# Block-masked attention with a mixture of experts: the scores of twelve attention units as three products of parts on 64 rows of the array per head

## Chip, cores and metric

The kernel runs on one core of one Trainium2 chip. The metric is the device time of one execution in microseconds (us), given as the median of several runs.

## What is computed

Block-masked attention over q, k and v of shape (4, 8, 576, 64): four batches, eight heads, 576 positions, 64 elements per head. The result, 2304 tokens of 512 features, goes through four experts that all work on every token, each with its own weight in the sum.

```python
scores = q @ k.T / sqrt(64)              # per batch and head, 576 x 576
mask = (pos_i // 64) >= (pos_j // 64)    # a query sees the keys of its own and earlier 64-blocks
attn = softmax(where(mask, scores, -1e9))
x = (attn @ v), heads side by side       # 2304 x 512
p = domain_probs / (sum(domain_probs) + 1e-9)
out = sum over e of p[:, e] * (relu(x @ w1[e]) @ w2[e])   # w1 512 x 1024, w2 1024 x 512
```

Everything is float32 outside. Inside, most products run on values that are split into two parts: a copy rounded to the type fp32r, the high part, and what the subtraction leaves, the low part. A product is then the sum of high by high, high by low and low by high.

## The kernel before, in words

**Order of the work.** Nothing is scheduled by hand. Each piece of work is a Python generator that asks for buffers and yields operations with a cost, an engine (or a choice of ACT and DVE) and a priority; `Flow.run` (line 212) takes the operation that can start first by these estimated times and appends it to its engine's program. So the order on each engine is fixed when the program is built, and at run time an engine waits in line for whatever its next instruction needs. An operation marked `late(..., by)` (line 382) is put later by a lag: `LAG_FIRST` 800 ns or `LAG` 3000 ns, so that TensorE doesn't reach it before its operands are there. The PE takes matmuls of the experts (`mm1` at line 1196, L1210; `mm2` at line 1238, L1261) between the operations of attention.

**Attention units.** After a first block of 64 queries per batch (`first_block`) there are 16 units (`unit`, line 455): four per batch, each with two heads, 512 queries (64 to 575) and 576 keys. The first four, those of batch 0, are "plain": their scores are float32 products with each head on 64 rows of the array, head 0 in partitions 0 to 63, head 1 in 64 to 127 (line 587). A float32 product leaves two passes in the trace. The twelve later units, "split", are what the change is about. Scores are made transposed, keys on the partitions and queries along the free axis, in pieces of 128 keys, each for the queries that see them: 512, 448, 320 and 192 queries wide, and 64 for the last 64 keys.

**Scores of a split unit before.** The k of both heads is turned by DVE into kT, head 0 in the upper half of the partitions and head 1 in the lower (L482). `k_thread` writes from it the tile KK: for each head, 128 rows of which 64 hold the high part of k and 64 the low part (lines 490 to 498). q is loaded twice, so that both halves of the partitions hold the same head, turned (L516) and split into HH (high) and LL (low), 1024 columns for two heads (lines 524 and 525). A piece is then two products on all 128 rows: KK by HH and KK by LL (lines 599 and 600), which add up high and low of k by high and low of q. The last 64 keys of both heads are one further product of 128 columns (lines 648 and 649). Each goes to one of two PSUM banks named att; the masked corners are overwritten with a large negative number (ACT L546 or DVE L548), then ACT or DVE copies the bank to the tile S (L703, L409), DVE takes the maximum into cm (L416), and the bank is free.

**After the scores.** GpSimd reduces cm over the partitions (L771), DVE subtracts, ACT takes the exponential (L727), DVE adds up the pieces, GpSimd sums over the partitions (L750). The products with v of two units run together (L825), in column halves of the array, into both att banks. The result is scaled, split and written to the experts' input x, or for the last two batches kept raw in the tiles xr, from which `prepare` (line 1315) makes the operands (A22, S3, S2, S1, S4) of the last two blocks. These two blocks are done in one go with a seven-product scheme (L1650, L1535).

Of the kernel before, what the change touches and what calls it, by code (L numbers as in the profile page):

```python
# [8 lines left out]
F32 = mybir.dt.float32  # L9
# [253 lines left out]
def kernel(  # L263
# [78 lines left out]
    for tag, n, shape, dt in (  # L342
        ("kr", 2, [P, S], F32),
        ("qr", 1, [P, 2 * MAXW], F32),
        ("kT", 1, [P, S], F32),
        ("qT", 1, [P, 2 * MAXW], F32),
        ("KK", 2, [P, 2 * S], F32R),
        ("HH", 1, [P, 2 * MAXW], F32R),
        ("LL", 1, [P, 2 * MAXW], F32R),
        ("VN", 2, [P, (MASK_BLOCK + MAXW) // P + 1, 3, D], F32),  # L350
        ("tr", 1, [P, MAXW], F32),
        ("tc", 1, [P, MAXW // 8], F32),
        ("S", 2, [P, 2 * MAXC], F32),
        ("cm", 1, [P, 2 * MAXW], F32),
        ("mx", 1, [P, 2 * MAXW], F32),
        ("sa", 1, [P, 2 * MAXW], F32),
        ("sb", 1, [P, 2 * MAXW], F32),
        ("xs", 2, [P, MAXW], F32),
        ("rc", 1, [P, MAXW], F32),
    ):  # L360
        bufs(tag, n, shape, dt, attn)
        counts[tag] = n
# [92 lines left out]
    def unit(u, ua, us, ju, pu, ph, job, dst, c):  # L455
        b, q0, q1 = job
        W = q1 - q0
        nt, odd = q1 // P, (q1 // MASK_BLOCK) % 2
# [9 lines left out]
        def k_thread():  # L468
# [16 lines left out]
            if plain:  # L485
                st["k"] = (kT, [t], [t])
                return
            KK = yield fl.take("KK", us)
            kt, kk = kT.tile, KK.tile
            a1 = yield a_copy(kk[0:64, :q1], kt[0:64, :q1], q1, [t], [kT, KK], pr)  # L490
            l1 = yield tt(BOTH, kk[64:128, :q1], kt[0:64, :q1], kk[0:64, :q1], SUB, q1, [a1], [kT, KK], pr)
            rot = MASK_BLOCK * odd
            second = []
            for to, of, n in ((q1 + rot, 0, q1 - rot), (q1, q1 - rot, rot)):
                if n:
                    second.append((yield a_copy(kk[64:128, to:to + n], kt[64:128, of:of + n], n, [t], [kT, KK], pr)))
                    second.append((yield tt(BOTH, kk[0:64, to:to + n], kt[64:128, of:of + n], kk[64:128, to:to + n],
                                            SUB, n, second[-1:], [kT, KK], pr)))
            fl.give(kT)
            st["k"] = (KK, [a1, l1], second)  # L500

        def q_thread():
# [4 lines left out]
            for h, j in ((h, j) for h in range(2) for j in range(2 if plain else 4)):  # L507
                p0, c0 = (64 * h + 32 * j, 0) if plain else (32 * j, h * W)
                vals.append((yield dma(
                    qr.tile[p0:p0 + 32, c0:c0 + W].rearrange("c (i r) -> c i r", r=32),  # L510
                    q[b, h0 + h, q0:q1, 32 * (j % 2):32 * (j % 2) + 32].rearrange("(i c) r -> c i r", c=32),
                    W * 128, u=[qr], prio=pr, packet=128)))
            yield ("until", lambda: left_first[0] == 0 and past["w"] > 2)
            qT = yield fl.take("qT", ua)
            n = W if plain else 2 * W
            t = yield op("dve", 1.04 * n + 70, lambda _: nc.vector.transpose(out=qT.tile[:, :n], in_=qr.tile[:, :n]),  # L516
                         vals, [qr, qT], pr)
            fl.give(qr)
            if plain:
                st["q"] = (qT, t)  # L520
                return
            HH = yield fl.take("HH", us)
            LL = yield fl.take("LL", us)
# [3 lines left out]
            st["q"] = (HH, LL, a, l)  # L527

        def v_thread():
# [11 lines left out]

        def mask(r, o, m, pb):

            def fn(e):
                if e == "act":
                    nc.scalar.activation(o, ident[r:r + 64, :64], AF.Copy, bias=neg, scale=0.0)  # L546
                else:
                    nc.vector.memset(o, neg)  # L548

            return op([("act", 193.0), ("dve", 120.0)], 0, fn, [m], [pb], pr - 1.0)  # L550

        banks = []
        for h in range(2):
            cur, used = [], 0
            for pc in pcs:
                if pc[0] is None and not plain:
                    continue
# [7 lines left out]
        if plain:  # L565
            banks.sort(key=lambda x: (x[1][0][0], x[0]))
        elif odd:
            banks.append((None, [pcs[-1]]))

        def s_thread():  # L570
# [6 lines left out]
            KK, ka, kb = st["k"]  # L577
            lag = LAG_FIRST if plain else LAG
            if plain:
                qT, qv = st["q"]  # L580
                Q = [qT]
                need = lambda h: ka + [qv]
                cost = lambda w: 2 * max(107.0, 2 * w / 2.4 + 2.5)

                def product(o, h, k0, n, lo):
                    hp = slice(64 * h, 64 * h + 64)
                    nc.tensor.matmul(out=o, lhsT=KK.tile[hp, k0:k0 + n], rhs=qT.tile[hp, lo:W], start=True, stop=True)  # L587
            else:
                HH, LL, qa, ql = st["q"]
                Q = [HH, LL]  # L590
                Hv = HH.tile[:, :2 * W].rearrange("p (h w) -> p h w", h=2)
                Lv = LL.tile[:, :2 * W].rearrange("p (h w) -> p h w", h=2)
                need = lambda h: (ka + kb if h is None else kb if h else ka) + [qa, ql]
                cost = lambda w: 2 * max(85.0, w / 2.4 + PEO)

                def product(o, h, k0, n, lo):
                    at = k0 + (q1 + MASK_BLOCK * odd) * h
                    hs = h
                    nc.tensor.matmul(out=o, lhsT=KK.tile[:, at:at + n], rhs=Hv[:, hs, lo:W], start=True, stop=False)  # L599
                    nc.tensor.matmul(out=o, lhsT=KK.tile[:, at:at + n], rhs=Lv[:, hs, lo:W], start=False, stop=True)  # L600

            for h, ps_list in banks:
                if plain:

                    if h:
                        continue
                    two = []
                    for _ in range(2):
                        two.append((yield fl.take("att", None, bank_tag)))

                    def fn(_, two=two, ps_list=ps_list):
                        at = 0
                        for j, a, w, _ in ps_list:
                            for g in range(2):
                                product(two[g].tile[:, at:at + w], g, q1 - P if j is None else P * j, P, a - q0)
                            at += w

                    ws = [x[2] for x in ps_list]
                    m = yield late(op("pe", 300.0 + (2 * sum(ws) + ws[0] - sum(abs(x - y) for x, y in zip(ws, ws[1:]))) / 1.2,
                                 fn, need(0), [*two, KK] + Q, pr), lag)  # L620
                    for g in range(2):
                        done, at, spots = [m], 0, {}
                        for j, a, w, _ in ps_list:
                            r = 64 if j is None else 128 if a == P * j else None
                            if r:
                                spots.setdefault(r, []).append(at)
                            at += w
                        for r, x in spots.items():
                            o = two[g].tile[r - 64:r, x[0]:x[0] + 64]
                            if len(x) == 2:  # L630
                                o = two[g].tile[r - 64:r, x[0]:2 * x[1] - x[0]].rearrange("p (n w) -> p n w", n=2)[:, :, :64]
                            i = ident[r - 64:r, :64 * len(x)]
                            i = i.rearrange("p (n w) -> p n w", n=2) if len(x) == 2 else i
                            done.append((yield op("act", 0.833 * 64 * len(x) + 140, lambda _, o=o, i=i: nc.scalar.activation(
                                o, i, AF.Copy, bias=neg, scale=0.0), [m], [two[g]], pr)))
                        st["banks"].append((g, ps_list, two[g], done))
                    continue
                pb = yield fl.take("att", None, bank_tag)
                ps = pb.tile
                use = [pb, KK] + Q  # L640
                done = []
                if h is None:
                    lo = W - MASK_BLOCK
                    n = 2 * MASK_BLOCK

                    def fn(_, ps=ps, n=n, lo=lo):
# [1124 lines left out]
```

## Time and profile before

| | |
|---|---|
| median of 3 runs | 880.06 us (879.18 to 880.15) |
| the profiled execution | 879.1 us, of it 877.3 us from its first to its last instruction |
| TensorE busy | 868.6 us of 877.3 |
| VectorE, ScalarE, GpSimd busy | 804.7, 551.0, 224.8 us |
| granted TensorE clock | 1.0 throughout |

Engines are PE (TensorE's matmuls), PEld (its weight loads), DVE (VectorE), ACT (ScalarE), POOL (GpSimd) and SP. A matmul's start is recorded, its end is modelled, so that successive matmuls overlap in the trace: the time that one costs is the step from its start to the start of the next, not its duration. In a form such as `64*128 64x512 f32` the first pair is the rows and columns of the array in use, the second the partitions and columns of the moving operand. fp32r is shown as f32 on PE.

### The profile page before, as it was taken

To read this page: it belongs to the slowest core of one execution; us is meant where nothing else is said; L and a number is where in the kernel's file an instruction comes from. 1 tells how busy PE (TensorE), PEld (TensorE's weight loads), DVE (VectorE), ACT (ScalarE), POOL (GpSimd) and SP (SyncE) were. 2 spreads that over 40 slices of the span, in tenths; PEclk is the share of its full clock that TensorE was granted. 3 is DMA by queue.
4 is the path that set the end of the run, shared out by engine and by line. 5 is a ranking of instruction groups with operands and counts; after the bars stand their busy time and mean duration, and the time that the engine had idled before them with its cause. 6 is when DMAs were issued, how large, how long until landed. Compare 5 with 4: busy or idle time off the path is not lost.

```text
span 877.3 us, 14545 instructions
## 1 busy us (share of the span) xinstructions
PE 868.6 (99%) x4965; PEld 729.1 (83%) x4967; DVE 804.7 (92%) x1489; ACT 551.0 (63%) x1183; POOL 224.8 (26%) x149
## 2 busy tenths in 40 slices
PE   8999999999999999999999999999999999999998
PEld 6777788878877887887887887889999999999998
DVE  6999999898898988988998789999999999999988
ACT  6696767765655564765764652585857677584852
POOL 1141100412412322232232322000061514334150
PEclk9999999999999999999999999999999999999999
DMA  7877457635455356356525223223383947575485
GB/s 172 220 183 213 133 129 194 167 125 122 97 125 140 81 132 147 110 135 149 111 66 152 65 89 91 85 82 112 96 127 69 142 79 125 94 137 72 74 125 165
DMA packets 231179, 108.10 MB, mean 123 GB/s; under 512 B 128448, under 2 KB 212416, under 8 KB 231104
## 3 DMA queue, kind: packets, MB, share of 16 engines
q1 hardware_dynamic: 215264, 93.13, 40.0%
q0 software_dynamic: 13824, 12.59, 12.0%
q10 hardware_dynamic: 2016, 1.44, 0.5%
q8 instruction: 39, 0.64, 0.3%
q14 instruction: 36, 0.29, 0.1%
HBM read 87.72 MB, written 19.40 MB: 122 GB/s over the span
## 4 chain that ended last, share of the span: by engine, by line
PE 95%; SPq 1%; ACT 1%; DMA 1%; issue 0%; DVE 0%; DVEq 0%; ACTq 0%
PE acc L1261 25%; PE h L1210 25%; PE acc L1535 18%; PE h L1650 10%; PE att L1650 8%; PE att L825 5%; PE att L600 2%; PE att L599 2%; SPq L394 1%; PE acc L587 1%; DMA qr<-in_q_dram 0%; PE att L587 0%; PE acc L825 0%; DMA w2r<-in_moe_w_dram 0%; DMA S<-in_k_dram 0%
## 5 line engine op out<-in xcount | busy, mean ns | idle before, releaser
L1210 PE MATMUL h<-xh,w1h 128*128 128x512 f32 (+1 forms) x384 | 137.2, 357 | 0.0
L1210 PE MATMUL h<-xh,w1l 128*128 128x512 f32 (+1 forms) x384 | 136.2, 355 | 0.0
L1210 PE MATMUL h<-xl,w1h 128*128 128x512 f32 (+1 forms) x384 | 136.0, 354 | 0.0
L750 POOL PARTITION_ALL_REDUCE sb<-sa x26 | 84.0, 3278 | 171.0 <-DVE tr L865 99.8
L1261 PE MATMUL acc<-w2h,hh 128*128 128x512 f32 x312 | 124.2, 398 | 0.0
L1261 PE MATMUL acc<-w2h,hl 128*128 128x512 f32 x312 | 122.0, 391 | 0.7 <-DVE hl L1230 0.7
L1261 PE MATMUL acc<-w2l,hh 128*128 128x512 f32 x312 | 122.0, 391 | 0.0
L409 ACT CAST w2h<-w2r 128x512 fp32r<-128x512 f32 (+1 forms) x114 | 70.0, 614 | 66.0 <-PE acc L1261 51.9
L771 POOL PARTITION_ALL_REDUCE mx<-cm x16 | 52.8, 3297 | 222.0 <-DVE cm L416 174.9
L1228 ACT ACTIVATE hh<-h 128x512 fp32r<-128x512 f32 (+1 forms) x94 | 49.2, 523 | 66.1 <-PE h L1210 65.8
L416 DVE TENSOR_TENSOR w1l<-w1r,w1h 128x512 fp32r<-128x512 f32 (+1 forms) x128 | 88.7, 695 | 1.9 <-ACT w1h L409 1.1
L403 POOL DMA_DIRECT2D out_dram<-ohp x48 | 42.6, 1393 | 161.2 <-DVE ohp L1571 161.2
L409 ACT CAST w1h<-w1r 128x512 fp32r<-128x512 f32 (+1 forms) x111 | 67.7, 611 | 23.9 <-DMA w1r<-in_moe_w_dram 15.0
L416 DVE TENSOR_TENSOR w2l<-w2r,w2h 128x512 fp32r<-128x512 f32 (+1 forms) x116 | 80.0, 691 | 2.7 <-ACT w2h L409 2.6
L1210 PEld LDWEIGHTS h<-xh,w1h 128*128 128x128 f32 x384 | 72.6, 189 | 11.3 <-issue 0.9
L1210 PEld LDWEIGHTS h<-xl,w1h 128*128 128x128 f32 x384 | 72.6, 189 | 10.2
L1210 PEld LDWEIGHTS h<-xh,w1l 128*128 128x128 f32 x384 | 72.5, 189 | 10.2
L1261 PEld LDWEIGHTS acc<-w2h,hl 128*128 128x128 f32 x312 | 58.6, 188 | 13.9 <-DVE hl L1230 1.2
L1261 PEld LDWEIGHTS acc<-w2h,hh 128*128 128x128 f32 x312 | 58.8, 188 | 13.4 <-issue 1.2
L1230 DVE SCALAR_TENSOR_TENSOR hl<-h,hh 128x512 fp32r<-128x512 f32 (+1 forms) x94 | 55.7, 593 | 13.7 <-ACT hh L1228 13.2
L1261 PEld LDWEIGHTS acc<-w2l,hh 128*128 128x128 f32 x312 | 58.9, 189 | 9.8
L403 POOL DMA_DIRECT2D out_dram<-o x48 | 42.5, 1382 | 76.7 <-DVE o L1571 63.4
(365 smaller groups left out, 2371.6 us busy)
## 6 DMA issues: line engine op xcount, KB each, us to landing
w1r<-in_moe_w_dram SPq DMA_DIRECT2D x120, 256.0 KB, 3.1
w2r<-in_moe_w_dram SPq DMA_DIRECT2D x116, 256.0 KB, 3.0
qr<-in_q_dram SPq DMA_DIRECT2D x112, 64.0 KB, 2.3
out_dram<-ohp POOLq DMA_DIRECT2D x48, 128.0 KB, 4.1
out_dram<-o POOLq DMA_DIRECT2D x48, 128.0 KB, 4.3
kr<-in_k_dram SPq DMA_DIRECT2D x64, 72.0 KB, 2.9
VN<-in_v_dram SPq DMA_DIRECT2D x32, 128.0 KB, 2.7
w2rp<-in_moe_w_dram SPq DMA_DIRECT2D x12, 256.0 KB, 3.4
```

What stands on the lines that cost most here:

```text
L403: o = op("pool", 1400.0, lambda _: nc.gpsimd.dma_start(out=dst, in_=src, accum_op=ALU.add), r, u, prio)
L409: o = op(engs, 0, lambda e: nc.scalar.copy(dst, src) if e == "act" else nc.vector.tensor_copy(dst, src), r, u, prio)
L416: o = op(engs, 0, lambda e: ENG[e].tensor_tensor(out=dst, in0=a, in1=b, op=alu), r, u, prio)
L750: sums.append((yield held(2300.0, op("pool", 150 + 6.3 * W, lambda _, h=h: nc.gpsimd.partition_all_reduce(sb.tile[:, h * W:h * W + W], sa. ...
L771: lambda _: nc.gpsimd.partition_all_reduce(mx.tile[:, :2 * W], src, P, RED.max),
L825: nc.tensor.matmul(out=x.tile[64 * g:64 * g + 64, W - w:W], lhsT=lhsT, rhs=rhs, start=(i == 0), stop=(i == len(todo) - 1))
L1210: nc.tensor.matmul(out=ps[:, :n], lhsT=s.tile[:, ks], rhs=x.tile[:, kc, :n], start=(kc == 0 and m == 0), stop=(kc == KC - 1 and m == 2),)
L1228: a = yield op("act", 0.833 * n + 55, lambda _: nc.scalar.activation(hh.tile[:, :n], ps[:, :n], AF.Relu), [mm], [pb, hh], 0.0)
L1230: l = yield op("dve", 1.04 * n + 70, lambda _: nc.vector.scalar_tensor_tensor(out=hl.tile[:, :n], in0=ps[:, :n], scalar=0.0, in1=hh.tile[: ...
L1261: nc.tensor.matmul(out=acc, lhsT=s.tile[:, ts], rhs=w.tile, start=(f == 0 and m == 0), stop=(f == FC - 1 and m == 2))
L1535: nc.tensor.matmul(out=acc[:, to], lhsT=s.tile[:, ts], rhs=v.tile[:, of], start=(start and first and m == 0 and k % 2 == 0), stop=(what != ...
L1650: nc.tensor.matmul(out=ps[:, :n], lhsT=w.tile[:, ks], rhs=x[:, kc, :n], start=(start and kc == 0 and m == 0), stop=(i in (2, 3, 4) and kc ...
```

## The change

Split units now make their scores the way plain ones do, but with parts. kT is split whole into KH and KL (128 partitions, one head in each half); q is loaded once per head, turned and split into QH and QL, 512 columns instead of 1024. Each piece is three products per head, KH by QH, KL by QH and KH by QL, on the 64 rows of the head; the two heads' products are issued alternately, into two att banks, which are both taken before the first product. The pieces come in the plain order, in three banks per head: 512; 192 and 320; 448 and 64. The last 64 keys become a full piece of 128 keys whose upper half is masked, so the last piece of v is loaded with 128 rows per head. Corners are masked by ACT alone, two in one instruction where a bank has two corners at the same partitions. The joint bank for the last 64 keys is gone.

```diff
 for tag, n, shape, dt in (
-    ("qr", 1, [P, 2 * MAXW], F32), ("qT", 1, [P, 2 * MAXW], F32),
-    ("KK", 2, [P, 2 * S], F32R), ("HH", 1, [P, 2 * MAXW], F32R), ("LL", 1, [P, 2 * MAXW], F32R),
+    ("qr", 1, [P, MAXW], F32), ("qT", 1, [P, MAXW], F32),
+    ("KH", 2, [P, S], F32R), ("KL", 2, [P, S], F32R),
+    ("QH", 2, [P, MAXW], F32R), ("QL", 2, [P, MAXW], F32R),
...
-        pcs, C = pieces_beside(q0, q1) if plain else pieces_of(q0, q1)
+        pcs, C = pieces_beside(q0, q1)
...
-            a1 = yield a_copy(kk[0:64, :q1], kt[0:64, :q1], q1, [t], [kT, KK], pr)
-            l1 = yield tt(BOTH, kk[64:128, :q1], kt[0:64, :q1], kk[0:64, :q1], SUB, q1, [a1], [kT, KK], pr)
...
+            a = yield a_copy(KH.tile[:, :q1], kT.tile[:, :q1], q1, [t], [kT, KH], pr)
+            l = yield tt(BOTH, KL.tile[:, :q1], kT.tile[:, :q1], KH.tile[:, :q1], SUB, q1, [a], [kT, KH, KL], pr)
...
-            for h, j in ((h, j) for h in range(2) for j in range(2 if plain else 4)):
+            for h, j in ((h, j) for h in range(2) for j in range(2)):
...
-            a = yield a_copy(HH.tile[:, :2 * W], qT.tile[:, :2 * W], 2 * W, [t], [qT, HH], pr)
-            l = yield tt(BOTH, LL.tile[:, :2 * W], qT.tile[:, :2 * W], HH.tile[:, :2 * W], SUB, 2 * W, [a], [qT, HH, LL], pr)
+            a = yield a_copy(QH.tile[:, :W], qT.tile[:, :W], W, [t], [qT, QH], pr)
+            l = yield tt(BOTH, QL.tile[:, :W], qT.tile[:, :W], QH.tile[:, :W], SUB, W, [a], [qT, QH, QL], pr)
...
-                r, o, n = (slice(0, P), 2 * h, P) if plain else (slice(64 * h, 64 * h + 64), 1, MASK_BLOCK)
-                jv.append((yield dma(VJ.tile[r, at, o, :], v[b, h0 + h, q1 - n:q1], n * 256, u=[VJ], prio=pr + 0.005, packet=256)))
+                jv.append((yield dma(VJ.tile[:, at, 2 * h, :], v[b, h0 + h, q1 - P:q1], P * 256, u=[VJ], prio=pr + 0.005, packet=256)))
...
+            turns = ((0, 0),) if plain else ((0, 0), (1, 0), (0, 1))
+            def product(two, at, k0, w, lo):
+                for i, (x, y) in enumerate(turns):
+                    for g in range(2):
+                        hp = slice(64 * g, 64 * g + 64)
+                        nc.tensor.matmul(out=two[g].tile[:, at:at + w], lhsT=K[x].tile[hp, k0:k0 + P], rhs=Q[y].tile[hp, lo:W],
+                                         start=(i == 0), stop=(i == len(turns) - 1))
...
-                        m = yield late(op("pe", cost(w), fn, need(h), use, pr), lag)
+                cost = 300.0 + (...) / 1.2 if plain else sum(3 * (x / 2.4 + PEO) for x in ws)
+                m = yield late(op("pe", cost, fn, ka + qv, [*two, *K, *Q], pr), lag)
```

## Rows read from the trace of the kernel before

**Rows 1.** The page: its head and the engines' busy time.

```profile
span 877.3 us, 14545 instructions
PE 868.6 (99%) x4965; PEld 729.1 (83%) x4967; DVE 804.7 (92%) x1489; ACT 551.0 (63%) x1183; POOL 224.8 (26%) x149
```

**Rows 2.** The chain that ended last, share of the span by engine.

```profile
PE 95%; SPq 1%; ACT 1%; DMA 1%; issue 0%; DVE 0%; DVEq 0%; ACTq 0%
```

**Rows 3.** The stretch 130 to 570 us: busy time and count of each engine, clock.

```profile
130.00:570.00 440.00, 440.00 (x2100) 355.23 (x2099) 395.85 (x652) 258.73 (x544) 117.32 (x36) 1.00 0.46 119
```

**Rows 4.** Waits of the weight loads, 130 to 570 us: total us, times, longest.

```profile
PEld acc L1261 <- ACT KK L409: 0.8, 1, 0.8
```

**Rows 5.** The products of all score pieces, by line: count, duration ns, first and last start.

```profile
L599 PE MATMUL att<-HH,KK x96: 251/334/393, 140.1 to 505.3; 128*128 128x512 f32 x24, 128*128 128x448 f32 x24, 128*128 128x320 f32 x24, 128*128 128x192 f32 x24
L649 PE MATMUL att<-LL,KK x12: 275/276/277, 154.5 to 508.3; 128*128 128x128 f32 x12
```

**Rows 6.** The chain in order of time: start us, us, twelve expert products in a row.

```profile
137.50 2.72 PE h L1210 x12
```

**Rows 7.** PE in order of time, first split unit: start us, us, what.

```profile
140.06 0.39 PE L599 MATMUL att<-HH,KK 128*128 128x512 f32 x1
...
141.15 0.40 PE L1261 MATMUL acc<-w2l,hh 128*128 128x512 f32 x1
...
143.65 0.30 PE L599 MATMUL att<-HH,KK 128*128 128x320 f32 x1
...
144.39 0.39 PE L1210 MATMUL h<-xl,w1h 128*128 128x512 f32 x1
...
154.44 0.22 PE L648 MATMUL att<-HH,KK 128*128 128x128 f32 x1
...
154.90 0.39 PE L1261 MATMUL acc<-w2l,hh 128*128 128x512 f32 x1
```

**Rows 8.** PE in order of time around two score groups of plain units.

```profile
61.14 0.39 PE L1261 MATMUL acc<-w2h,hl 128*128 128x512 f32 x1
61.46 1.13 PE L587 MATMUL acc<-qT,kT 64*128 64x192 f32 x8
...
62.86 0.40 PE L1261 MATMUL acc<-w2l,hh 128*128 128x512 f32 x1
...
83.12 0.40 PE L1261 MATMUL acc<-w2h,hl 128*128 128x512 f32 x1
83.44 1.13 PE L587 MATMUL acc<-qT,kT 64*128 64x512 f32 x4
...
85.76 0.39 PE L1261 MATMUL acc<-w2l,hh 128*128 128x512 f32 x1
```

**Rows 9.** Weight loads in order of time, in such a group and around L649.

```profile
83.44 0.30 PEld L587 LDWEIGHTS acc<-qT,kT 64*128 64x128 f32 x4 [0.36 <-ACT rc L844]
83.98 0.19 PEld L587 LDWEIGHTS att<-qT,kT 64*128 64x128 f32 x2 [0.23 <-ACT xs L409]
84.41 0.20 PEld L587 LDWEIGHTS att<-qT,kT 64*128 64x128 f32 x2 [0.23 <-issue]
...
154.55 0.19 PEld L1261 LDWEIGHTS acc<-w2h,hh 128*128 128x128 f32 x1
154.66 0.19 PEld L1261 LDWEIGHTS acc<-w2l,hh 128*128 128x128 f32 x1
```

**Rows 10.** Groups of DVE, 130 to 570 us: count, busy us, mean ns.

```profile
L416 DVE TENSOR_TENSOR LL<-qT,HH 128x1024 fp32r<-128x1024 f32 x12 | 19.0, 1581 | 0.2
...
L416 DVE TENSOR_TENSOR KK<-kT,KK 64x576 fp32r<-64x576 f32 x11 | 10.0, 910 | 0.3
```

**Rows 11.** DMA issues of q: count, KB each, us to landing.

```profile
qr<-in_q_dram SPq DMA_DIRECT2D x112, 64.0 KB, 2.3
```

**Rows 12.** In order of time: when S3l is made on DVE and first read on PE.

```profile
546.76 1.22 DVE L416 TENSOR_TENSOR S3l<-xr,S3h 128x1024 fp32r<-128x1024 f32 x1
...
555.08 0.39 PE L1650 MATMUL h<-S3l,w1hp 128*128 128x512 f32 x1
```

More of the change, by code (lines that the diff above doesn't have):

```diff
@@ L485, in k_thread @@
             if plain:
-                st["k"] = (kT, [t], [t])
+                st["k"] = ((kT,), [t])
                 return
-            KK = yield fl.take("KK", us)
-            kt, kk = kT.tile, KK.tile
-            a1 = yield a_copy(kk[0:64, :q1], kt[0:64, :q1], q1, [t], [kT, KK], pr)
-            l1 = yield tt(BOTH, kk[64:128, :q1], kt[0:64, :q1], kk[0:64, :q1], SUB, q1, [a1], [kT, KK], pr)
[L492 to L498, printed above, removed]
+            KH = yield fl.take("KH", us)
+            KL = yield fl.take("KL", us)
+            a = yield a_copy(KH.tile[:, :q1], kT.tile[:, :q1], q1, [t], [kT, KH], pr)
+            l = yield tt(BOTH, KL.tile[:, :q1], kT.tile[:, :q1], KH.tile[:, :q1], SUB, q1, [a], [kT, KH, KL], pr)
             fl.give(kT)
-            st["k"] = (KK, [a1, l1], second)
+            st["k"] = ((KH, KL), [a, l])
         def q_thread():
@@ L514, in q_thread @@
             qT = yield fl.take("qT", ua)
-            n = W if plain else 2 * W
-            t = yield op("dve", 1.04 * n + 70, lambda _: nc.vector.transpose(out=qT.tile[:, :n], in_=qr.tile[:, :n]),
+            t = yield op("dve", 1.04 * W + 70, lambda _: nc.vector.transpose(out=qT.tile[:, :W], in_=qr.tile[:, :W]),
                          vals, [qr, qT], pr)
@@ L555, in unit @@
             for pc in pcs:
-                if pc[0] is None and not plain:
-                    continue
                 if used + pc[2] > 512:
@@ L564, in unit @@
                 banks.append((h, cur))
[L565 to L568, printed above, removed]
+        banks.sort(key=lambda x: (x[1][0][0], x[0]))
         def s_thread():
@@ L576, in s_thread @@
             st["banks"] = []
-            KK, ka, kb = st["k"]
             lag = LAG_FIRST if plain else LAG
[L579 to L600, printed above, removed]
@@ L602, in s_thread @@
-            for h, ps_list in banks:
[L603 to L636, printed above, removed]
-                    continue
[L638 to L646, printed above, removed]
-                        lhsT = KK.tile[:, q1 - MASK_BLOCK:q1 + MASK_BLOCK]
-                        nc.tensor.matmul(out=ps[:, :n], lhsT=lhsT, rhs=Hv[:, :, lo:W], start=True, stop=False)
-                        nc.tensor.matmul(out=ps[:, :n], lhsT=lhsT, rhs=Lv[:, :, lo:W], start=False, stop=True)
-                    m = yield late(op("pe", 220.0, fn, need(None), use, pr), lag)
-                    m1 = yield mask(64, ps[64:128, 0:64], m, pb)
-                    m2 = yield mask(0, ps[0:64, 64:128], m, pb)
-                    done = [m, m1, m2]
-                else:
@@ new lines, in s_thread @@
+            K, ka = st["k"]
+            Q, qv = st["q"]
+            turns = ((0, 0),) if plain else ((0, 0), (1, 0), (0, 1))
[5 more added lines that the diff above has]
+                                         start=(i == 0), stop=(i == len(turns) - 1))
@@ L656, in s_thread, with fn @@
+            for h, ps_list in banks:
+                if h:
+                    continue
+                two = []
+                for _ in range(2):
+                    two.append((yield fl.take("att", None, bank_tag)))
+                def fn(_, two=two, ps_list=ps_list):
                     at = 0
-                    corners = []
                     for j, a, w, _ in ps_list:
-                        def fn(_, o=ps[:, at:at + w], j=j, h=h, a=a):
-                            product(o, h, P * j, P, a - q0)
-                        m = yield late(op("pe", cost(w), fn, need(h), use, pr), lag)
-                        done = [m]
-                        if a == P * j:
-                            corners.append(at)
-                        at += w
@@ L668, in s_thread @@
-                    for x in corners:
-                        done.append((yield mask(64, ps[64:128, x:x + 64], done[0], pb)))
-                st["banks"].append((h, ps_list, pb, done))
-            fl.give(KK, *Q)
+                        product(two, at, q1 - P if j is None else P * j, w, a - q0)
+                        at += w
+                ws = [x[2] for x in ps_list]
+                cost = 300.0 + (2 * sum(ws) + ws[0] - sum(abs(x - y) for x, y in zip(ws, ws[1:]))) / 1.2 if plain else sum(3 * (x / 2.4 + PEO) for x in ws)
@@ new lines, in s_thread @@
+                m = yield late(op("pe", cost, fn, ka + qv, [*two, *K, *Q], pr), lag)
+                for g in range(2):
+                    done, at, spots = [m], 0, {}
+                    for j, a, w, _ in ps_list:
+                        r = 64 if j is None else 128 if a == P * j else None
+                        if r:
+                            spots.setdefault(r, []).append(at)
+                        at += w
+                    for r, x in spots.items():
+                        o = two[g].tile[r - 64:r, x[0]:x[0] + 64]
+                        if len(x) == 2:
+                            o = two[g].tile[r - 64:r, x[0]:2 * x[1] - x[0]].rearrange("p (n w) -> p n w", n=2)[:, :, :64]
+                        i = ident[r - 64:r, :64 * len(x)]
+                        i = i.rearrange("p (n w) -> p n w", n=2) if len(x) == 2 else i
+                        done.append((yield op("act", 0.833 * 64 * len(x) + 140, lambda _, o=o, i=i: nc.scalar.activation(
+                            o, i, AF.Copy, bias=neg, scale=0.0), [m], [two[g]], pr - (0.0 if plain else 1.0))))
+                    st["banks"].append((g, ps_list, two[g], done))
@@ L673, in e_thread @@
+            fl.give(*K, *Q)
         def e_thread():
@@ L682, in e_thread @@
                 cu = [] if alone else [cm]
-                if h is None:
-                    _, a, w, c0 = ps_list[0]
-                    pv = ps[:, :2 * w].rearrange("p (h w) -> p h w", h=2)
-                    e = yield a_copy(Sv[:, :, c0:c0 + w], pv, 2 * w, done, [pb, Sb], pr, True)
-                    st["evac"].append(e)
-                    if not alone:
-                        base = Sv[:, :, a - q0:W] if len(pcs) == 2 else cv[:, :, a - q0:W]
-                        st["evac"].append((yield tt("dve", cv[:, :, a - q0:W], pv, base, MAX, 2 * w, done + st["evac"],
-                                                    [pb, Sb] + cu, pr)))
-                else:
-                    tot = sum(x[2] for x in ps_list)
-                    c0 = ps_list[0][3]
-                    moves = [(Sv[:, h, c0:c0 + tot], ps[:, :tot])]
-                    r1 = min([x[1] for x in pcs[1:]], default=q0) - q0
-                    if r1 and ps_list[0][0] == 0:
-                        moves.append((cv[:, h, :r1], ps[:, :r1]))
-                    n = tot + r1 * (len(moves) - 1)
-                    def fn(e, moves=moves):
-                        for d_, s_ in moves:
-                            (nc.scalar.copy if e == "act" else nc.vector.tensor_copy)(d_, s_)
-                    e = yield op([("act", 0.833 * n + 60 * len(moves)), ("dve", 1.04 * n + 70 * len(moves))], 0, fn, done,
-                                 [pb, Sb] + cu, pr - (0.0 if plain else 1.0))
-                    st["evac"].append(e)
-                    at = 0
-                    for j, a, w, _ in ps_list:
-                        r = a - q0
-                        if j == 0:
-                            pass
-                        else:
-                            base = Sv[:, h, r:W] if j == 1 else cv[:, h, r:W]
-                            st["evac"].append((yield tt("dve", cv[:, h, r:W], ps[:, at:at + w], base, MAX, w,
-                                                        done + st["evac"], [pb, Sb] + cu, pr)))
-                        at += w
@@ new lines, in e_thread, with fn @@
+                tot = sum(x[2] for x in ps_list)
+                c0 = ps_list[0][3]
+                moves = [(Sv[:, h, c0:c0 + tot], ps[:, :tot])]
+                r1 = min([x[1] for x in pcs[1:]], default=q0) - q0
+                if r1 and ps_list[0][0] == 0:
+                    moves.append((cv[:, h, :r1], ps[:, :r1]))
+                n = tot + r1 * (len(moves) - 1)
+                def fn(e, moves=moves):
+                    for d_, s_ in moves:
+                        (nc.scalar.copy if e == "act" else nc.vector.tensor_copy)(d_, s_)
@@ new lines, in e_thread @@
+                e = yield op([("act", 0.833 * n + 60 * len(moves)), ("dve", 1.04 * n + 70 * len(moves))], 0, fn, done,
+                             [pb, Sb] + cu, pr - (0.0 if plain else 1.0))
+                st["evac"].append(e)
+                at = 0
+                for j, a, w, _ in ps_list:
+                    r = a - q0
+                    if j == 0:
+                        pass
+                    else:
+                        base = Sv[:, h, r:W] if j == 1 else cv[:, h, r:W]
+                        st["evac"].append((yield tt("dve", cv[:, h, r:W], ps[:, at:at + w], base, MAX, w,
+                                                    done + st["evac"], [pb, Sb] + cu, pr)))
+                    at += w
@@ L820, in fn @@
                                 if x is all_two[n]:
-                                    lhsT = VJ.tile[:, j, 2 * g, :] if j is not None else VJ.tile[:, nj, 2 * g if plain else 1, :]
+                                    lhsT = VJ.tile[:, j, 2 * g, :] if j is not None else VJ.tile[:, nj, 2 * g, :]
                                     rhs = PJ.tile[:, g * C + c0:g * C + c0 + w]
```

34 lines of the change are left out of this document (14 added, 20 removed).

## The prediction

> **What bounds the kernel now.** First the page: PE is busy 99% of the span, far ahead of the others [rows 1]. Busy time alone proves little for PE, since its ends are modelled, so the chain that ended last comes next: 95% of it is PE [rows 2]. Then the stretch in which all twelve split units lie, 130 to 570 us: PE is busy for all of its 440 us, at full clock, while DVE has 44 us and ACT 181 us to spare [rows 3]. Last the waits there: the one instruction outside attention whose load waited for another engine did so for 0.8 us, under a running matmul [rows 4]. So in that stretch time is the sum of PE's steps. What the change takes from DVE, ACT or the queues is worth nothing by itself; what it adds to or takes from PE's steps counts in full.
>
> **What the split scores cost now.** A step is the distance between two starts. A 512-column product of the experts takes 2.72 / 12 = 0.227 [rows 6]. The cost of a run of score products is the time from its first start to the second expert product behind it, less one such step; in this way a slow start of the follower is charged to the scores. 512 and 448 columns, two products each: 1.09 - 0.227 = 0.863. 320 and 192: 0.74 - 0.227 = 0.513. The joint one of 128 columns: 0.46 - 0.227 = 0.233 [rows 7]. The second head has the same shapes, and every unit the same counts (24 of each width, 12 of the joint one) [rows 5]. One unit: 2 x (0.863 + 0.513) + 0.233 = 2.985; twelve: 35.8 us.
>
> **What they will cost: streaming.** New are 15 steps per unit, each a pair of 64-row products, one per head. Plain units show such pairs, in two-pass float32: one pass over 512 columns, for both heads, takes 0.43 (83.98 to 84.41) [rows 9], which is 1024 clock periods at 2.4 GHz; so the heads do run side by side. One-pass fp32r on 64 rows isn't in this trace. On 128 rows, fp32r takes 0.227 for 512 columns [rows 6], 0.013 over columns / 2.4 GHz. I take that sum for a pair of any width. Bounds: nothing beyond the columns, as in the float32 pass (15 x 0.013 = 0.20 less per unit), or 0.013 for either head (0.20 more). A step also can't be shorter than a weight load: loads that follow one another without a pause start 0.11 apart (154.55, 154.66) [rows 9]. The two heads' loads go together: four of them take 0.30 [rows 9], two rounds 0.11 apart and one load's 0.19. So per unit: 512: 3 x 0.227 = 0.681. 192 and 320: 3 x 0.110 + 3 x 0.146 = 0.768. 448 and 64: 3 x 0.200 + 2 x 0.110 + 0.040 = 0.860. Sum 2.309, which is 0.68 less than now.
>
> **What they will cost: the change of array shape.** Before, scores and experts both used 128 x 128. Now each bank pair is an island of 64-row products among 128-row ones. The trace has such islands. The one at 61.46: from the expert product ahead of it (61.14) to the second one behind (62.86) are 1.72; less two normal steps 1.266; its streaming is 2 passes x (192 + 320) x 2 / 2.4 GHz = 0.853. So 0.41 goes to neither. The one at 83.44: 2.64 - 0.454 = 2.186; streaming 2 x 0.427 + 2 x 0.373 + 0.110 + 0.053 = 1.763, which leaves 0.42 [rows 8]. I read the parts as follows: 0.09 before the first 64-row load may start (83.44 - 83.12 - 0.227), 0.11 in which the first load hides behind nothing, and the same again on the way out. I take 0.42; the two islands and their rounding put it between 0.38 and 0.46. How many islands? A group needs both att banks, and there are only two, so no two groups can touch, nor can one touch a product with v, which takes both too: 3 per unit, 36 in all. 3 x 0.42 = 1.26 per unit.
>
> **Sum on PE.** 2.309 + 1.26 = 3.569 against 2.985: +0.584 per unit, +7.0 us for twelve.
>
> **The rest, costed at nothing, with its cover.** DVE: the low part of q falls from 1024 to 512 columns, 0.8 less; of the subtractions for k, 576 columns each for either head on 64 partitions, one on 128 stays, 0.91 less [rows 10]; over twelve units about 20 us, and half of q's transpose on top, less a few us for maxima that are taken per head instead of jointly. ACT: fewer copies, 72 corner masks instead of 96. SP: q is issued four times per unit instead of eight, 48 of the 112 issues fewer [rows 11], so nothing is moved past another queue; 24 loads of v double from 16 to 32 KB. None of these was late for PE [rows 4], so their relief buys nothing, and the v loads keep as cover the whole softmax between scores and product. Without PE as the bound the 20 us of DVE would count. Outside 130 to 570 us the plain units' code is unchanged.
>
> **A wait that is added.** A group's first load now waits for two free banks and for all four parts; before, each run of products needed one bank and head 0's began without head 1's k. Behind it on PE stand the experts' products, and behind those everything. The order is built with 3 us of lag for just this, and the same lag left PE without a wait so far [rows 4]; I cost it at nothing and keep it as a rival. The late end of the units has slack as well: S3l is finished at 547.98 and first read at 555.08 [rows 12], so the chain may end 7 us later before PE notices.
>
> **Rivals.**
>
> Rival 1, not slower: the shape change is cheaper for one-pass fp32r than in the two-pass rows, because loads are pulled forward past it. Break-even is at (2.985 - 2.309) / 3 = 0.23 per island; at zero the twelve units give back 8.1 us, 872.0. For it: fp32r islands aren't in the trace. Against: the 0.09 and the first load are paid before the first product, whatever its type. The Trainium skill's span model (TensorE: Matmul & The Clock Gate, section "Measured speedup vs the span model") gives a pack of tiles the time of one matmul and some 4 ns per further tile, with nothing for entering or leaving; taken alone it leads to this rival. The trace agrees with it inside a group and not at its edges.
>
> Rival 2, slower still: PE stands in line for the second bank. A turn of the banks needs masks, two copies and the maxima of both heads; if 0.3 us were missing at half of the 36 groups, 5 us more, 892. Against it: the lag of 3 us. The Trainium skill (TensorEngine Tiling (Array Packing), "Gotcha 1: PSUM Pressure") holds that row tiles need banks of their own; that is the pairwise taking of banks here, and no run so far shows its price.
>
> Rival 3: fp32r pairs don't overlap, each head streams by itself: 4608 further columns per unit, 1.92 us, 23 us in all, 910. Against: the float32 pairs.
>
> **The numbers.** The profiled execution took 879.1 us, 1.8 more than its span; the sum makes 886.1 of it. The median of the runs is 0.96 higher, so 880.06 + 7.0 = 887.1. The forecast's own range, with its bounds of 0.20 per unit (2.4 us) and 0.04 per island (1.4 us), is 883.3 to 890.9. Chances: forecast 0.70, rival 1 0.17 (faster 0.12, about even 0.05), rival 2 0.09, rival 3 0.04. A measurement of this kernel tells about 0.2%, 1.8 us, from no change. Slower: 0.70 + 0.09 + 0.04 = 0.83; same 0.05; faster 0.12. The range reaches down to no change and up to rival 2, 880 to 893, and leaves out faster, rival 3 and the worst of rival 2, under 0.2.
>
> **What would show it.** Right: from 130 us on, the expert product behind each island starts some 0.1 late, and the one after it again; islands of 6, 12 and 12 products cost near 1.10, 1.19 and 1.28 by the reckoning above; 512-column pairs step by 0.227; PE still has no wait, and the stretch is 7 us longer with DVE some 20 us less busy. Wrong: pair steps near 0.43 for 512 columns (rival 3), a weight load that waits for ACT or DVE (rival 2), or edges well under 0.2 (rival 1).

## The result, and the profile after

The changed kernel takes 887.24 us (median of 4 runs, 886.36 to 887.86) against 879.62 (878.76 to 880.15) for the kernel before on the same chip: a ratio of 1.0087, 95% interval 1.0069 to 1.0104. 7.0 us were forecast, 7.6 measured.

The page, and the stretch of the split units; its end is set 7 us later than in [rows 3], so that it holds about the same work. Columns as in [rows 1] and [rows 3]:

```profile
span 885.6 us, 14738 instructions
PE 875.5 (99%) x5111; PEld 720.0 (81%) x5111; DVE 791.1 (89%) x1487; ACT 522.4 (59%) x1113; POOL 224.5 (25%) x149
```

```profile
130.00:577.00 447.00, 447.00 (x2250) 346.01 (x2247) 382.45 (x650) 232.21 (x478) 116.69 (x36) 1.00 0.43 111
```

PE is as full as before and the others are emptier: DVE by 13 us against [rows 3], ACT by 27. So the loss should lie in PE's steps. One unit, PE in order of time (start us, us, what):

```profile
159.47 0.39 PE L1127 MATMUL h<-xh,w1l 128*128 128x512 f32 x1
159.79 0.51 PE L563 MATMUL att<-QH,KH 64*128 64x512 f32 x2
160.13 0.40 PE L563 MATMUL att<-QH,KL 64*128 64x512 f32 x2
160.36 0.40 PE L563 MATMUL att<-QL,KH 64*128 64x512 f32 x2
160.69 0.50 PE L1178 MATMUL acc<-w2h,hh 128*128 128x512 f32 x1
161.03 0.40 PE L1178 MATMUL acc<-w2l,hh 128*128 128x512 f32 x1
...
164.68 0.39 PE L1127 MATMUL h<-xh,w1l 128*128 128x512 f32 x1
164.99 0.47 PE L563 MATMUL att<-QH,KH 64*128 64x448 f32 x2
...
166.39 0.39 PE L1127 MATMUL h<-xl,w1h 128*128 128x512 f32 x1
...
173.42 0.39 PE L1178 MATMUL acc<-w2h,hl 128*128 128x512 f32 x1
173.74 0.35 PE L563 MATMUL att<-QH,KH 64*128 64x192 f32 x2
...
175.05 0.39 PE L1178 MATMUL acc<-w2l,hh 128*128 128x512 f32 x1
```

Each line "x2" is a pair, both heads within 0.01 us. The island of 512 columns shows all four parts of what an island costs beyond its streaming. A normal step after 159.47 would end at 159.70; the first pair starts at 159.79 (0.09). Its step is 0.34 where the next is 0.23 (0.11 for a load that nothing hides). After the last pair, 160.36 + 0.227 would be 160.59; the expert product starts at 160.69 (0.10), and its step is 0.34 again (0.11). By the reckoning of the prediction the three islands cost 1.56 - 0.454 = 1.11, 1.71 - 0.454 = 1.26 and 1.63 - 0.454 = 1.18. The same sum over all 36 is 42.4 us, 3.54 per unit; over the 72 runs of score products before it is 35.9 us, 2.99 per unit. That is 6.5 of the 8.3 us between the two profiled spans. About 1 us more had already gone before the first split unit: the last product with v of the plain units starts at 127.66 instead of 126.61. That point lies anywhere from 126.1 to 128.3 in the thirteen profiles of this study, though the plain units' code is the same in all, so it is taken as scatter. 0.4 us is a wait near 640 us (0.1 before). The last 0.4 us or so is not traced.

The waits of the weight loads in that stretch (total us, times, longest):

```profile
PEld att L563 <- issue: 9.9, 28, 0.4
...
PEld att L563 <- ACT w1h L410: 1.1, 3, 0.4
PEld acc L1178 <- ACT QH L410: 0.8, 1, 0.8
```

Two weight loads in order of time, the first of an island and the one behind it:

```profile
159.79 0.19 PEld L563 LDWEIGHTS att<-QH,KH 64*128 64x128 f32 x2 [0.35 <-issue]
159.90 0.19 PEld L563 LDWEIGHTS att<-QH,KL 64*128 64x128 f32 x2
```

The 0.35 us of idle load path ahead of an island is its edge again: the first load starts together with the first pair, and not under the product ahead, as the second one does. PE is busy through all 447 us of the stretch, so no engine made it wait there.

### The profile page after: what moved, and what is told of

Read it like the earlier page. It is cut to its first block, busy times and chain, and to the rows that moved or that the text cites. A ratio compares the mean times of both kernels' runs of the same rounds, so it can differ in the third digit from the quotient of the medians.

```text
span 885.6 us, 14738 instructions
## 1 busy us (share of the span) xinstructions
PE 875.5 (99%) x5111; PEld 720.0 (81%) x5111; DVE 791.1 (89%) x1487; ACT 522.4 (59%) x1113; POOL 224.5 (25%) x149
## 4 chain that ended last, share of the span: by engine, by line
PE 94%; ACT 3%; SPq 1%; DMA 1%; issue 1%; DVE 0%; DVEq 0%; ACTq 0%
PE acc L1178 25%; PE h L1127 25%; PE acc L1452 17%; PE h L1567 10%; PE att L1567 7%; PE att L742 5%; PE att L563 4%; SPq L395 1%; PE acc L563 1%; DMA qr<-in_q_dram 1%; PE acc L742 0%; DMA w2r<-in_moe_w_dram 0%; DMA S<-in_k_dram 0%; ACT ohp L1482 0%; ACT w1h L410 0%
## 5 line engine op out<-in xcount | busy, mean ns | idle before, releaser
L410 ACT CAST w2h<-w2r 128x512 fp32r<-128x512 f32 (+1 forms) x111 | 68.1, 614 | 70.4 <-PE acc L1178 58.5
L417 DVE TENSOR_TENSOR w1l<-w1r,w1h 128x512 fp32r<-128x512 f32 (+1 forms) x128 | 90.9, 714 | 2.6 <-ACT w1h L410 1.8
L417 DVE TENSOR_TENSOR w2l<-w2r,w2h 128x512 fp32r<-128x512 f32 (+1 forms) x116 | 82.9, 716 | 10.4 <-ACT w2h L410 10.0
L410 ACT CAST w1h<-w1r 128x512 fp32r<-128x512 f32 (+1 forms) x108 | 65.9, 611 | 15.7 <-DMA w1r<-in_moe_w_dram 7.1
```

The source lines that it names most:

```text
L410: o = op(engs, 0, lambda e: nc.scalar.copy(dst, src) if e == "act" else nc.vector.tensor_copy(dst, src), r, u, prio)
L417: o = op(engs, 0, lambda e: ENG[e].tensor_tensor(out=dst, in0=a, in1=b, op=alu), r, u, prio)
```

## The experiments

Eleven kernels. "Changed" is 887.24 us, measured with the result; "before" is 879.5 to 879.8 on the chips of the experiments.

### Taking away the change of shape alone

```diff
                 for i, (x, y) in enumerate(turns):
+                    if not plain:
+                        nc.tensor.matmul(out=two[i // 2].tile[:, at:at + w], lhsT=K[x].tile[:, k0:k0 + P], rhs=Q[y].tile[:, lo:W],
+                                         start=(i != 1), stop=(i != 0))
+                        continue
                     for g in range(2):
...
```

> The changed kernel, but the split units' three products of a piece run on all 128 rows, one instruction where there was a pair: KH by QH and KL by QH into the first bank, KH by QL into the second. The heads are thereby summed in the scores (part of the computation that is changed). The columns streamed per step, the loads, the banks, the waits and the order of the program stay; only the change of array shape is gone. Theory (an island of 64-row products costs 0.42 us for entering and leaving): 36 islands go, a unit costs near 2.35 us instead of 3.54, so 14 us less than the changed kernel, 873, and some 7 less than the kernel before. Rival (the loss lies in the streams, in taking two banks or in the wait for all parts): still near 887.

Measured: 873.69 us, ratio to before 0.9932 (0.9910 to 0.9953); 13.6 less than changed. The same three products on 128 rows, PE in order of time:

```profile
157.02 0.39 PE L1131 MATMUL h<-xh,w1l 128*128 128x512 f32 x1
157.25 0.39 PE L562 MATMUL att<-QH,KH 128*128 128x512 f32 x1
157.47 0.39 PE L562 MATMUL att<-QH,KL 128*128 128x512 f32 x1
157.70 0.39 PE L562 MATMUL att<-QL,KH 128*128 128x512 f32 x1
157.93 0.39 PE L1182 MATMUL acc<-w2h,hh 128*128 128x512 f32 x1
158.15 0.39 PE L1182 MATMUL acc<-w2l,hh 128*128 128x512 f32 x1
...
162.75 0.28 PE L562 MATMUL att<-QL,KH 128*128 128x64 f32 x1
162.86 0.48 PE L1131 MATMUL h<-xh,w1h 128*128 128x512 f32 x1
163.18 0.40 PE L1131 MATMUL h<-xl,w1h 128*128 128x512 f32 x1
```

1.13 - 0.454 = 0.68 where the island took 1.11: same steps of 0.23, no edges. Over the 36 groups the trace gives 28.8 us instead of 42.4. Banks, waits and operands are as in the changed kernel, so the cost of the edges is the shape's. It is 13.6 / 36 = 0.38 in the mean: the groups of 512 and of 192 and 320 columns lose 0.42 and 0.40, the one of 448 and 64 only 0.31. Behind its steps of 64 columns the next expert product is slow without any change of shape too (0.32 from 162.86 to 163.18, instead of 0.23).

### Adding an island

```diff
-                if used + pc[2] > 512:
+                if used + pc[2] > 512 or (not plain and pc[0] is None):
...
-        banks.sort(key=lambda x: (x[1][0][0], x[0]))
+        banks.sort(key=lambda x: ((x[1][0][0], 9)[x[1][0][0] is None], x[0]))
```

> The changed kernel with the last piece of 64 queries in a bank pair and a group of its own, so four islands per unit instead of three, and the same products. Theory (the price is per island): 12 more islands at 0.42, 5.0 us more, 892.2. Rival (the price hangs on the products, not on how often the array changes shape): 887. Second rival (banks taken in pairs are what PE will wait for, and a fourth turn makes it wait): more than 5 us, with weight loads that wait for ACT or DVE in the trace.

Measured: 907.09 us, ratio 1.0308 (1.0291 to 1.0325), 20 more than changed instead of 5. The islands themselves did as expected (0.41 us more per unit, 4.9 in all). The rest is elsewhere, in the waits of PE (total us, times, longest) and in a stretch behind the last unit:

```profile
PE att L1567 <- DVE S3h L410: 9.5, 1, 9.5
...
PE acc L1452 <- DVE xl L417: 1.0, 1, 1.0
PE acc L1452 <- ACT xh L410: 0.8, 1, 0.8
...
PE att L1567 <- DVE S3l L417: 0.6, 1, 0.6
```

```profile
566.00:584.00 18.00, 7.88 (x20) 5.59 (x20) 17.49 (x26) 4.09 (x8) 0.53 (x1) 0.62 0.14 44
```

The units end late: the last score product starts at 542.7 us, in the changed kernel at 512.1. The operands of the last two blocks are made after the units by a busy DVE, PE stands still for 9.5 us, and the granted clock averages 0.62 in this stretch. The islands' 4.9, waits of 11.9 and 2.4 us of slow clock (last section) are 19 of the 20 us. The second rival had the wait right and its place wrong: not at the banks but at the hand-over of S3h and S3l from DVE to PE, to which the prediction gave 7 us of slack. So the same kernel with shorter turns of the banks:

```diff
-LAG, LAG_PV = 3000.0, 3000.0
+LAG, LAG_PV = 1500.0, 3000.0
```

> The run with a fourth island per unit, and the lag with which a group of score products is put behind its operands cut from 3000 to 1500 ns. In the run with 3000 the islands cost 0.41 us each more, as expected, and PE waited 9.7 us and ran at half clock behind it, since the units ended late. Theory (the turns of the bank pairs, with the lag in each, set when the units end): four turns are 6 us shorter per unit, the wait for S3h goes or falls under 2 us, and what stays is the islands' 5 us, near 892. Rival (DVE sets the end): the wait stays, near 907.

Measured: 891.79 us, ratio 1.0139 (1.0122 to 1.0156), 4.6 more than changed. The wait for S3h is gone. PE's longest is one near 22 us, before any split unit, which the other kernels have too in some size:

```profile
PE acc L1178 <- DVE hl L1147: 1.0, 1, 1.0
```

With the end out of the way twelve more islands cost 4.6 us, 0.38 each; 4.9 by the trace, 0.41 each. The changed kernel with the shorter lag and three islands was not run, so the 4.6 takes it that the lag by itself costs PE nothing; the 4.9 doesn't need that.

### Are the heads side by side, and does their order matter?

```diff
-                        hp = slice(64 * g, 64 * g + 64)
+                        hp = slice(64 * g, 64 * g + 64) if plain else slice(0, 64)
```

> The changed kernel with the products of both heads of a split unit on rows 0 to 63 (head 1's scores are made from head 0's k and q, so that part of the computation is changed). Same products, same islands, but no two can run side by side. Theory (the two heads of a pair overlap fully): every one of the 15 steps is paid twice, 2.3 us more per unit, 27 to 28 us in all, near 915. Rival (the pairs shown side by side in the trace in fact share the stream): no change, 887.

Measured: 915.71 us, 28.5 more than changed; 1.0407 (1.0388 to 1.0426) of before. Pairs overlap fully: without it the islands cost 29.0 us more by the trace, 2.4 per unit. Their edges stay as they were, so these don't come from two heads running at once.

```diff
-                for i, (x, y) in enumerate(turns):
-                    for g in range(2):
+                for g in range(2):
+                    for i, (x, y) in enumerate(turns):
```

> The changed kernel with the order of the six products of a piece turned round: the three of head 0, then the three of head 1, instead of alternating. Same products, same islands. Theory (the two heads run side by side only where they are neighbours in program order): four slots per piece instead of three and one more at a group's end, 1.2 us more per unit, 14 to 15 us in all, near 902. Rival (fp32r pairs don't overlap anyway, the streams are paid per head): no change, 887.

Measured: 887.11 us, ratio 1.0088 (1.0065 to 1.0111): no change. The expectation fell, but not for the rival's reason, which the run with shared rows excludes. The program now lists three products of head 0 first; the trace shows

```profile
158.60 0.51 PE L563 MATMUL att<-QH,KH 64*128 64x512 f32 x2
158.94 0.41 PE L563 MATMUL att<-QH,KL 64*128 64x512 f32 x2
159.17 0.40 PE L563 MATMUL att<-QL,KH 64*128 64x512 f32 x2
```

the two heads again pairwise, at most 0.02 us apart. Head 1's first product starts ahead of two of head 0's that stand before it in the program. How far this goes:

```diff
-            def product(two, at, k0, w, lo):
+            def product(two, at, k0, w, lo, heads=(0, 1)):
...
-                    for g in range(2):
+                    for g in heads:
...
-                    at = 0
-                    for j, a, w, _ in ps_list:
-                        product(two, at, q1 - P if j is None else P * j, w, a - q0)
-                        at += w
+                    for heads in ((0, 1),) if plain else ((0,), (1,)):
+                        at = 0
+                        for j, a, w, _ in ps_list:
+                            product(two, at, q1 - P if j is None else P * j, w, a - q0, heads)
+                            at += w
```

> The changed kernel with all products of head 0 of a bank pair issued first, then all of head 1: six and six where there were twelve alternating ones, three and three for the 512 columns. After the run with the order turned round within a piece: theory now (each half of the rows takes its products in its own order, whatever stands between them in the program): no change, 887, and head 1's first product starts within 0.02 us of head 0's in the trace. Rival (only a few instructions are looked ahead): head 1 starts late, up to 1.8 us more per unit, 22 in all.

Measured: 896.86 us, ratio 1.0193 (1.0174 to 1.0212), 9.6 more than changed. It lies between the two theories: groups of three and three products are as quick as before (1.10), those of six and six 0.52 and 0.31 slower. In one of the latter

```profile
166.36 0.47 PE L563 MATMUL att<-QH,KH 64*128 64x448 f32 x1
166.67 0.36 PE L563 MATMUL att<-QH,KL 64*128 64x448 f32 x1
166.87 0.36 PE L563 MATMUL att<-QL,KH 64*128 64x448 f32 x1
166.88 0.47 PE L563 MATMUL att<-QH,KH 64*128 64x448 f32 x2
```

head 1's first product starts beside head 0's third, 0.52 us late. (0.52 + 0.31) x 12 = 10 us is the measured loss.

### What a product is worth, with islands and without

```diff
-            turns = ((0, 0),) if plain else ((0, 0), (1, 0), (0, 1))
+            turns = ((0, 0),) if plain else ((0, 0), (1, 0))
```

> The changed kernel without the third product, KH by QL, of the split units (the low part of q is left out of the scores). Order of the program and islands stay. Theory (every step is paid in full, the wider of its stream and one load): 0.227 + 0.200 + 0.146 + 2 x 0.107 = 0.79 us less per unit, 9.4 us in all, 877.8, with islands of 0.87, 0.95 and 0.92. Rival (steps partly hide behind loads or drains, so the islands are dearer and the streams cheaper than I make them): clearly less than 9 us saved.

Measured: 877.32 us, ratio 0.9972 (0.9955 to 0.9989), 9.9 less than changed; islands of 0.86, 0.94 and 0.91. Steps are paid in full.

```diff
-                    nc.tensor.matmul(out=o, lhsT=KK.tile[:, at:at + n], rhs=Hv[:, hs, lo:W], start=True, stop=False)
-                    nc.tensor.matmul(out=o, lhsT=KK.tile[:, at:at + n], rhs=Lv[:, hs, lo:W], start=False, stop=True)
+                    nc.tensor.matmul(out=o, lhsT=KK.tile[:, at:at + n], rhs=Hv[:, hs, lo:W], start=True, stop=True)
...
-                        nc.tensor.matmul(out=ps[:, :n], lhsT=lhsT, rhs=Hv[:, :, lo:W], start=True, stop=False)
-                        nc.tensor.matmul(out=ps[:, :n], lhsT=lhsT, rhs=Lv[:, :, lo:W], start=False, stop=True)
+                        nc.tensor.matmul(out=ps[:, :n], lhsT=lhsT, rhs=Hv[:, :, lo:W], start=True, stop=True)
```

> The kernel before without the products KK by LL: each piece is one product on 128 rows instead of two (the low part of q is left out of the scores, as in the changed kernel with two products). Theory (steps on PE are paid in full, no islands): a unit costs 2 x (0.227 + 0.200 + 0.146 + 0.107) + 0.115 = 1.48 instead of 2.99, 18 us less than the kernel before, near 862. Rival (with PE 18 us shorter, DVE or the end of the units becomes the bound): less than 12 us saved, with a wait of PE for S3h or for an hl in the trace.

Measured: 863.24 us, ratio 0.9814 (0.9799 to 0.9830). 16.6 us less than before instead of 18. By the trace a unit costs 1.59 instead of the 1.48 expected; most units are near 1.5, and a few groups waited for ACT or DVE to empty their bank, 0.5 us at most. These last two kernels leave out the same part of the scores, the low part of q. The one that keeps high and low of k stacked on 128 rows, without islands, is 14 us ahead. It is the fastest of all here, for whoever can spare the low part of q. With all three terms nothing tried beats the kernel before.

### DVE's work, given back and added

```diff
             l = yield tt(BOTH, KL..., kT..., KH..., SUB, q1, [a], [kT, KH, KL], pr)
+            l = yield tt(BOTH, KL..., kT..., KH..., SUB, q1, [a, l], [kT, KH, KL], pr)
...
             l = yield tt(BOTH, QL..., qT..., QH..., SUB, W, [a], [qT, QH, QL], pr)
+            l = yield tt(BOTH, QL..., qT..., QH..., SUB, W, [a, l], [qT, QH, QL], pr)
```

> The changed kernel with the low parts of k and of q each subtracted twice in the split units, so that DVE gets back some 19 us of what the change took from it (0.91 and 0.69 us more per unit). PE's work stays. Theory (PE is the bound where the split units lie, DVE's relief is worth nothing there): within 1 us of the changed kernel, 887. Rival (part of DVE's relief was used, and hid that the islands cost still more): clearly slower, up to 19 us.

Measured: 900.00 us, ratio 1.0228 (1.0214 to 1.0242), 12.8 more than changed. PE's score steps are unchanged and PE is busy without a gap from 130 to 560 us; then

```profile
PE att L1569 <- DVE S3h L410: 6.7, 1, 6.7
```

the hand-over again. By the trace 17 us of subtractions were added (12 of 0.75 and 12 of 0.68), more than the 13 us by which the change had relieved DVE. Does that mean that DVE's relief had paid for the paired banks? A like load on the kernel before:

```diff
             l = yield tt(BOTH, LL..., qT..., HH..., SUB, 2 * W, [a], [qT, HH, LL], pr)
+            l = yield tt(BOTH, LL..., qT..., HH..., SUB, 2 * W, [a, l], [qT, HH, LL], pr)
```

> The kernel before with the low part of q subtracted twice in the split units: 1.58 us more of DVE per unit, 19 us in all, about what the changed kernel got back in the run with the subtractions doubled. There the units ended so late that PE waited some 9 us for S3h. Theory A (the taking of banks in pairs makes a unit's way longer, and DVE's relief paid for it): here the bank turns are short, the wait for S3h stays under 2 us and the time within 3 us of the kernel before. Theory B (any 19 us more on DVE bring the end of the units too late, pairs or not): a wait for S3h of over 5 us and more than 8 us slower.

Measured: 898.35 us, ratio 1.0216 (1.0201 to 1.0231), 19 more than before:

```profile
PE att L1651 <- DVE S3h L409: 13.6, 1, 13.6
```

Theory A falls: the kernel before, without paired banks, stumbles over added work too. The load was 12 subtractions of 1.22 us, 14.6 in all, and not the 19 expected: the mean of 1.58 in [rows 10] is made of eight of 1.22 and four of 2.2 to 2.5. And the changed kernel with both subtractions doubled and shorter turns:

> The changed kernel with both subtractions doubled, and the lag cut from 3000 to 1500 ns. Theory (the end of the units is set by the turns of the bank pairs together with DVE, and shorter turns make room for DVE's work): the wait for S3h falls under 2 us, near 888. Rival (DVE alone sets the end): the wait stays, near 900.

Measured: 889.57 us, ratio 1.0114 (1.0099 to 1.0129), 10.4 less than with the long lag; S3h is read 1.4 us after it is made and S3l 0.2 us: no wait for them is left, and hardly any slack. Its edit is the doubled subtractions and the one line of the lag, both shown above. So in the changed kernel when the units end is set by DVE's work and the planned lags together; for the kernel before the lag was not tried. The slack in the changed kernel:

```profile
554.87 1.22 DVE L417 TENSOR_TENSOR S3l<-xr,S3h 128x1024 fp32r<-128x1024 f32 x1
...
562.27 0.39 PE L1567 MATMUL h<-S3h,w1hp 128*128 128x512 f32 x1
```

S3l is finished at 556.09 and first read right behind S3h, at 562.50, 6.4 us later; before it was 7.1 [rows 12].

## Why the prediction was right

**What bounds the kernel.** Right: the stretch is PE's steps. Adding to them (shared rows), taking from them (two products, no islands) moved the time by what PE's steps in the trace add up to (28.5 for 29.0, 9.9 for 9.8, 13.6 for 13.6 us).

**Cost before.** 2.985 per unit forecast from one unit's rows, 2.99 over all twelve.

**Streaming.** Pairs of fp32r step like single products on 128 rows: 0.23 for 512, 0.20 for 448 columns, and 0.11 where a load is longer than the stream. The middle of three values was the true one; the run with shared rows shows the overlap to be complete. The prediction's ground for it was weaker than it reads: 1024 clock periods for two heads of 512 columns would also fit two streams of one column per period, one after the other.

**The change of shape.** 0.42 per island, read from islands of two-pass float32, held for one-pass fp32r: islands of 1.11, 1.18 and 1.26 (6, 12 and 12 products) against 1.10, 1.19 and 1.28. The run without islands puts 0.38 of it per island on the change of shape alone, the lower end of the forecast's 0.38 to 0.46; the streaming alone came out at 2.40 per unit against 2.309. Both misses are mainly the slow follower behind 64 columns, and they cancel in the sum. The run with a fourth island gives 0.38 to 0.41 for the whole of it (its streaming is not new), once its end was freed. Sum 3.54 against 3.569, so +6.5 us where 7.0 stood. The rest of the measured 7.6 is about the size of the scatter, so that the total came as near as 0.6 us is partly luck.

**Rival 1** fell to the run without islands: its 872 needed an edge that costs nothing, and 873.7 came only when the edges were gone. **Rival 3** fell to the overlap. **Rival 2**, a wait for the second bank, didn't come; but with one more turn per unit the time went to 907 by a wait at another place.

**The rest, costed at nothing.** No wait came of it in the changed kernel, so the step held for the number, and it was too simple. DVE was relieved by 13 us, not 20. The subtractions and turns of k and q did fall, from 54.7 to 25.6 us by their groups in the stretch. But other groups grew: the subtractions of the experts' weights from 93.3 to 99.0, the scalings into tc from 2.0 to 6.8, the copies of banks on DVE from 1.4 to 4.1; why is not shown. That the relief bought nothing isn't shown either. Without it the units of the changed kernel might have ended too late: 17 us more on DVE cost 12.8 us there, and no run gave back just the 13. In the kernel before 14.6 us more cost 18.8. The sentence on the slack (7 us at S3l) named the place; that it would run out so soon was not seen.

## What to carry to other kernels

Splitting the array among 64-row products pays only where a run of them saves more than its edges: each entry and exit among 128-row products costs 0.3 to 0.4 us together here. Count the islands first, then the columns: three islands per unit cost 1.1 us, and the narrower stream saved 0.6. Look for an island of the same shape in the trace you have; its edges can be read from four starts, and here they carried over from float32 to fp32r. And an engine off the critical path has a slack with an end: find the hand-over where it is used up before calling its work free.

## What the runs showed of the hardware that was not expected

A product on one half of the rows can start ahead of products on the other half that stand before it in the program, up to a point. With three products of head 0 listed ahead, head 1's first still started 0.01 us after head 0's first; with six ahead it started beside the third, 0.52 us late. After PE's standstill of 9.5 us in the run with a fourth island, the granted clock was at its lower level (0.50, 1.2 GHz) for a dozen products of 512 columns more, which took 0.43 instead of 0.23 each: 2.4 us on top of the wait.
